# w2 in 27 rows for every partition, and two more rows for the first 64 partitions

## The chip, the cores and the metric

The kernel runs on one core of a Trainium2 chip. The metric is the device time of one execution in microseconds (us); the time of the kernel before is the median of three runs. One execution more was taken with the hardware profiler; the profile, the trace behind it and all times inside the program come from that one.

## What is computed

One token for each of four sequences goes through a transformer layer in bfloat16: attention over the last 2048 positions of a cache, with 32 query heads on 4 key-value heads, then a gated feed-forward part. Cut to what matters:

```python
# x [4,1,1024]; wq [1024,4096]; wo [4096,1024]; w1, w3 [1024,3584]; w2 [3584,1024]
q = layernorm(x) @ wq                       # 32 heads of 128
p = softmax(q . k_cache[last 2048] * 128 ** -0.5)
h = x + (p . v_cache[last 2048]) @ wo
n = layernorm(h)
out = h + (silu(n @ w1) * (n @ w3)) @ w2
```

Each weight and each used row of the caches is read once, and there are only four rows of activations, so most of the work is moving 55.58 MB from HBM to SBUF.

## The kernel before

**Loads.** All large loads go through a ring of five slots of 32 KB for each partition (`NSLOT`, `SLOT`). The list `ring` (L107) gives their order: k in two pairs, half of wq, two slots without a load (for the transposed k), the other half of wq, v in two pairs, wo in two pairs, w1 in two halves, w3 in two halves, w2. `fill()` (L119 to L135) runs down this list and issues each load on SyncE's queue at L133, as far as the slot that it needs was released; `done()` marks a part as used and calls `fill()` again. So the loads stand in one queue in this order, and SyncE waits in it for what the slot's former readers have to finish. The order of all other instructions is the order in which the program writes them (`manual_schedule`).

**Layout of the weights.** wq, w1, w3 have row `p * 8 + kc` on partition p, four `kc` to a load. w2 has row `p * 28 + fc` on partition p (`w2_v`, L79), 28 rows for each, and is loaded in four transfers of 16, 8, 2 and 2 rows (`W2B`, L108): the first fills a slot, the other three share the last one. wo comes as four transfers of 2 MB (`wo_`, L101), two to a slot.

**Attention** (L234 to L424). TensorE transposes k; the projection by wq is made in four bands of 32 partitions (`tile_position`); then scores, row maxima, exponentials on ScalarE, a transpose of the weights on VectorE, and the product with v, pipelined over the four sequences.

**From wo to the end.** L434 multiplies with wo, 128 matmuls of 256 columns; L444 adds x; a second layernorm gives `hn_T`. `up_projection` (L450 to L466) makes for w1 and again for w3 64 matmuls of 448 columns: 8 `kc`, two halves `hf` of the columns, four bands `c`. Band c holds the columns `c * 896` to `c * 896 + 895`, so the result is two tiles of 128 x 448. L472 to L476 make silu of the first result from exp, add, reciprocal and multiply, before the second projection; L480 multiplies it with the second result. `transpose_quads` (L223) transposes the 128 x 896 product in 32 x 32 blocks on VectorE into `hg_T`, 28 blocks of 32 columns. L491 multiplies block fc with row fc of every partition's w2: 112 matmuls of 256 columns, which accumulate in one PSUM tile. L501 adds h, and two small transfers store the result, one on SyncE's queue and one on ScalarE's (L503, L504).

Of the kernel before, what the change touches and what calls it, by code (L numbers as in the profile page):

```python
# [10 lines left out]
P = 128  # L11
ACT = mybir.ActivationFunctionType
ALU = mybir.AluOpType
AX = mybir.AxisListType
BF16 = mybir.dt.bfloat16
FP32 = mybir.dt.float32
# [7 lines left out]
def kernel(  # L24
# [20 lines left out]
    nc = tc.nc  # L45

    B, _, D = A_x.shape
    Hkv, Sk, Dh = A_k_cache.shape[1], A_k_cache.shape[2], A_k_cache.shape[3]
    NQ = A_wq.shape[1]
    Hq = NQ // Dh  # L50
    REP = Hq // Hkv
    W = min(4096, max(256, Sk // 4))
    F = B_w1.shape[1]
    KC = D // P
    FC = F // P
    NK = W // P
    C = 4
    R = 32
    S = R // B
    DQ = D // C  # L60
    FQ = F // C
    FH = FQ // 2
    assert B == C and Hkv == C and B * Hq == P and Dh == P and REP * Hkv == R
    assert D == KC * P and F == FC * P and W == NK * P and NQ == Hq * Dh
    eps = 1e-5
    qscale = float(Dh) ** -0.5

# [3 lines left out]
    T = REP  # L71
# [4 lines left out]
    wo_v = A_wo.rearrange("(g p t) n -> p g (t n)", g=Hkv, t=T)  # L76
    w1_v = B_w1.rearrange("(p kc) f -> p kc f", kc=KC)
    w3_v = B_w3.rearrange("(p kc) f -> p kc f", kc=KC)
    w2_v = B_w2.rearrange("(p fc) n -> p fc n", fc=FC)  # L79

    const = ctx.enter_context(tc.tile_pool(name="const", bufs=1))
    act = ctx.enter_context(tc.tile_pool(name="act", bufs=1))
# [3 lines left out]
    ps = ctx.enter_context(tc.tile_pool(name="ps", bufs=1, space=bass.MemoryType.PSUM))  # L86
# [6 lines left out]
    def pair(parts):  # L93
        return [parts[0:2], parts[2:4]]
# [3 lines left out]
        for name, cache in (("k", A_k_cache), ("v", A_v_cache))  # L98
    )
    kT_ = pair([("kT", b, [JR, P], None) for b in range(B)])  # L100
    wo_ = pair([("wo", g, [1, T * D], wo_v[:, g : g + 1, :]) for g in range(Hkv)])  # L101

    def four_rows(name, view, n):
        return [[(name, i, [4, n], view[:, 4 * i : 4 * i + 4, :])] for i in range(KC // 4)]

    wq_ = four_rows("wq", wq_v, NQ)
    ring = k_ + wq_[:1] + kT_ + wq_[1:] + v_ + wo_ + four_rows("w1", w1_v, F) + four_rows("w3", w3_v, F)  # L107
    W2B = [16, 8, 2, 2]  # L108
    w2_ = []
    f0 = 0  # L110
    for i, n in enumerate(W2B):
        w2_.append(("w2", i, [n, D], w2_v[:, f0 : f0 + n, :]))
        f0 += n
    ring += [w2_[:1], w2_[1:]]
    views = {}
    taken = []
    used = set()
# [1 line left out]
    def fill():  # L119

        while len(taken) < len(ring):
            n = len(taken) - NSLOT
            if n >= 0 and not all((name, i) in used for name, i, _, _ in ring[n]):
                break
            parts = ring[len(taken)]
            slot = stream.tile([P, SLOT], BF16, tag="slot", name="s_" + parts[0][0])
            o = 0
            for name, i, shape, src in parts:
                dst = slot[:, o : o + int(np.prod(shape))]
                o += int(np.prod(shape))  # L130
                view = dst.rearrange("p (a b) -> p a b", a=shape[0])
                if src is not None:
                    nc.sync.dma_start(out=dst if name in ("k", "v") else view, in_=src)  # L133
                views[(name, i)] = view
            taken.append(slot)  # L135

    def get(name, i):
        return views[(name, i)]

    def done(name, i):  # L140
        used.add((name, i))
        fill()
# [5 lines left out]
    nc.vector.memset(x_nat[:], 0.0)  # L148
    nc.scalar.dma_start(out=x_nat[::S, :], in_=x_flat.rearrange("b (c n) -> c b n", c=C))
    fill()  # L150

    ident = const.tile([P, P], BF16)
# [8 lines left out]
        out=t32[:], in_=ident[:].rearrange("p (q h) -> p h q", q=C), axis=AX.X, op=ALU.add  # L161
# [4 lines left out]
    for q in range(C):  # L166
# [3 lines left out]
        out=negm[:], in_=t32[:].rearrange("p (g r) -> p g r", g=Hkv), axis=AX.X, op=ALU.add  # L170
    )
    nc.vector.tensor_scalar(
        out=negm[:], in0=negm[:], scalar1=-1.0, scalar2=-NEG, op0=ALU.add, op1=ALU.mult
# [3 lines left out]
        out=jmask[:, :, 0], in_=ident[:].rearrange("p (j h) -> p j h", j=JM), axis=AX.X, op=ALU.add  # L177
# [6 lines left out]
    for l in range(2):  # L184
        nc.gpsimd.tensor_copy(
            out=strip[:, l, B - 1 :].rearrange("p (c x) -> p c x", c=C)[:, :, : B * Hkv].rearrange(
                "p c (g b) -> p c g b", b=B
            )[:, :, :, 0],
            in_=t32[:].rearrange("p (g c l) -> p l c g", g=Hkv, c=C)[:, l],
        )  # L190

    def layernorm_T(h_T, tag):

# [29 lines left out]
    def transpose_quads(dst, src, n):  # L223

        nc.vector.transpose(
            out=dst.rearrange("p j r -> p (j r)"), in_=src.rearrange("p (q j) -> p j q", j=n)
        )
# [24 lines left out]
    for i in range(KC // 4):  # L252
        w = get("wq", i)
        for kk in range(4):
            kc = 4 * i + kk
            for hf in range(2):
                for c in range(C):
                    o = (2 * c + hf) * HALF * Dh
                    nc.tensor.matmul(  # L259
                        q_ps[hf][R * c : R * c + R],  # L260
                        lhsT=xn_T[:, kc, :],
                        rhs=w[:, kk, o : o + HALF * Dh],
                        start=(kc == 0),
                        stop=(kc == KC - 1),
                        tile_position=(0, R * c),
# [12 lines left out]
    for b in range(B):  # L278
        nc.vector.tensor_copy(  # L279
            out=Qm[:, b].rearrange("p (g y) -> p g y", y=QW)[:, :, :REP],  # L280
            in_=qT_ps[:, :, :, S * b].rearrange("p r g -> p g r"),
# [125 lines left out]
    for l in range(2):  # L407
        for b in range(B):
            nc.tensor.matmul(  # L409
                on_ps[:, l],  # L410
                lhsT=strip[:, l, B - 1 - b : B - 1 - b + P],
                rhs=om[:, b],
                start=(b == 0),
                stop=(b == B - 1),
# [8 lines left out]
        out=oP[:, :, :, ::S],  # L423
        in_=oX[:, :, : Hkv * B].rearrange("p t (g b) -> p g t b", b=B),  # L424
# [2 lines left out]

    y_ps = ps.tile([P, DQ], FP32, tag="kt0")
    for g in range(Hkv):
        w = get("wo", g)  # L430
        for t in range(T):
            for c in range(C):
                o = t * D + c * DQ
                nc.tensor.matmul(  # L434
                    y_ps[R * c : R * c + R, :],
                    lhsT=oP[:, g, t, :],
                    rhs=w[:, 0, o : o + DQ],
                    start=(g == 0 and t == 0),
                    stop=(g == Hkv - 1 and t == T - 1),
                    tile_position=(0, R * c),  # L440
                )
        done("wo", g)
    h1 = act.tile([P, DQ], FP32)
    nc.vector.tensor_tensor(out=h1[:], in0=y_ps[:], in1=x_nat[:], op=ALU.add)  # L444
    h_T = act.tile([P, KC, R], FP32)
# [1 line left out]
    hn_T = layernorm_T(h_T[:], "ln2")  # L447


    def up_projection(name, out_ps):  # L450
        for i in range(KC // 4):
            w = get(name, i)
            for kk in range(4):
                kc = 4 * i + kk
                for hf in range(2):
                    for c in range(C):
                        o = c * FQ + hf * FH
                        nc.tensor.matmul(  # L458
                            out_ps[hf][R * c : R * c + R],
                            lhsT=hn_T[:, kc, :],  # L460
                            rhs=w[:, kk, o : o + FH],
                            start=(kc == 0),
                            stop=(kc == KC - 1),
                            tile_position=(0, R * c),
                        )
            done(name, i)  # L466

    gu_ps = [ps.tile([P, FH], FP32, tag=f"sc{i}", name=f"gu_ps{i}") for i in range(4)]
    up_projection("w1", gu_ps[:2])
    eg = act.tile([P, 2, FH], FP32)  # L470
    for hf in range(2):
        nc.scalar.activation(out=eg[:, hf], in_=gu_ps[hf][:], func=ACT.Exp, scale=-1.0)  # L472
    nc.vector.tensor_scalar_add(out=eg[:], in0=eg[:], scalar1=1.0)
    nc.vector.reciprocal(out=eg[:], in_=eg[:])
    for hf in range(2):
        nc.vector.tensor_tensor(out=eg[:, hf], in0=gu_ps[hf][:], in1=eg[:, hf], op=ALU.mult)  # L476
    up_projection("w3", gu_ps[2:])
    hg = act.tile([P, 2, FH], BF16)
    for hf in range(2):
        nc.vector.tensor_tensor(out=hg[:, hf], in0=gu_ps[2 + hf][:], in1=eg[:, hf], op=ALU.mult)  # L480
    hg_T = act.tile([P, FC, R], BF16)
    transpose_quads(hg_T[:], hg[:].rearrange("p a f -> p (a f)"), FC)


    y2_ps = ps.tile([P, DQ], FP32, tag="kt1")
    fc = 0
    for i, n in enumerate(W2B):
        w = get("w2", i)
        for ff in range(n):
            for c in range(C):  # L490
                nc.tensor.matmul(  # L491
                    y2_ps[R * c : R * c + R, :],
                    lhsT=hg_T[:, fc, :],
                    rhs=w[:, ff, c * DQ : (c + 1) * DQ],
                    start=(fc == 0),
                    stop=(fc == FC - 1),
                    tile_position=(0, R * c),
                )
            fc += 1
    res = act.tile([P, DQ], BF16)  # L500
    nc.vector.tensor_tensor(out=res[:], in0=y2_ps[:], in1=h1[:], op=ALU.add)  # L501
    out_v = out_flat.rearrange("b (c n) -> c b n", c=C)
# [32 lines left out]
```

## Time and profile before

| what | value |
|---|---|
| time, median of 3 runs (lowest to highest) | 140.02 us (139.83 to 140.04) |
| the profiled execution's own time | 140.13 us |
| its span, first to last instruction | 138.3 us |
| its time outside the span | 1.83 us |
| read from HBM | 55.58 MB, 402 GB/s over the span |
| busy: PE, DVE, ACT, POOL | 80.2, 52.9, 42.7, 4.2 us |
| mean granted clock of TensorE | 0.781 |

How to read what follows. PE is TensorE's matmuls and PEld its weight loads, DVE is VectorE, ACT ScalarE, POOL GpSimd, SP SyncE; a q behind a name is the engine's instruction queue. The page cuts the span into 40 equal slices; a digit is a busy share in tenths, and GB/s is what the DMA engines moved in that slice. Queue lines give packets, MB and the share of sixteen DMA engines' span that the packets took. The chain that ended last is followed back from the last instruction; a row of it has start, length, engine and tile. A row of the timeline has start, length, engine, line, operation, output and inputs, shapes, number of instructions, and in brackets how long the engine stood idle before and what ended that. Behind the views stand the trace's single packets (queue, start, length, bytes) and, for each transfer, the times at which its closing signals arrived, one for each DMA engine that took part.

### The profile page before, as it was taken

The numbers are of one execution on the slowest core, as the hardware profiler recorded it, in microseconds if no ns is written. First come the engines' busy times: TensorE is split into PE (matmuls) and PEld (weight loads), VectorE is DVE, ScalarE is ACT, GpSimd is POOL, SyncE is SP. The second block draws the span as 40 slices with busy tenths as digits, with TensorE's granted clock in tenths as the row PEclk, the third lists the DMA queues.
The fourth block names the chain that finished last, engine by engine and source line by source line (L and its number), as shares of the span: only waits on it lengthen the run. The fifth ranks groups of instructions, "written<-read, shape, count | busy, mean of one in ns | idle before, by whom it ended". The sixth has DMA issues, their size and how long they took to land.

```text
span 138.3 us, 2012 instructions
## 1 busy us (share of the span) xinstructions
PE 80.2 (58%) x866; PEld 47.5 (34%) x868; DVE 52.9 (38%) x97; ACT 42.7 (31%) x57; POOL 4.2 (3%) x18
## 2 busy tenths in 40 slices
PE   0029898921903889328918998659539901703780
PEld 0029887820301322014304434537324400202550
DVE  3036676520000235177087197540330298350001
ACT  3005988850000325998807900000040200000000
POOL 7400000000000000000000000000000000000000
PEclk9999999998555799975797799965865896555555
DMA  4999999999989999999999999999999999999930
GB/s 152 399 423 431 431 436 455 455 441 398 445 384 426 441 417 417 450 407 431 450 400 431 433 469 431 394 448 448 419 398 448 456 411 430 445 407 398 406 148 2
DMA packets 3217, 55.72 MB, mean 403 GB/s; under 512 B 360, under 2 KB 392, under 8 KB 648
## 3 DMA queue, kind: packets, MB, share of 16 engines
q1 hardware_dynamic: 3178, 55.58, 94.4%
q8 instruction: 7, 0.11, 0.3%
q10 hardware_dynamic: 30, 0.01, 0.0%
q14 instruction: 2, 0.02, 0.0%
HBM read 55.58 MB, written 0.01 MB: 402 GB/s over the span
## 4 chain that ended last, share of the span: by engine, by line
DMA 49%; PE 27%; DVE 13%; ACT 4%; SPq 3%; issue 2%; DVEq 0%
DMA s_wq<-in_A_wq_dram 29%; DMA s_w<-in_B_w_dram 20%; PE o_ps L369 10%; PE y_ps L434 5%; ACT P L334 4%; PE sc_ps L294 3%; DVE PT L346 3%; SPq L133 3%; PE gu_ps L458 2%; PE q_ps L259 2%; DVE om L386 2%; DVE od L378 2%; PE on_ps L409 1%; PE tot_ps L355 1%; PE nm_ps L323 1%
## 5 line engine op out<-in xcount | busy, mean ns | idle before, releaser
L334 ACT ACTIVATE P<-sc_ps,bias 128x512 bf16<-128x512 f32 x16 | 19.7, 1417 | 9.6 <-DVE bias L331 9.6
L241 PE MATMUL kt_ps<-ident,s_k 128*128 128x128 bf16 x256 | 17.3, 228 | 1.3 <-ACT s_kT L245 1.0
L369 PE MATMUL o_ps<-s_v,PT 128*128 128x512 bf16 x62 | 17.5, 439 | 0.3 <-issue 0.2
L241 PEld LDWEIGHTS <-s_k 128*128 128x128 bf16 x256 | 16.3, 103 | 2.3 <-issue 1.7
L245 ACT COPY s_kT<-kt_ps 128x1024 bf16<-128x1024 bf16 x16 | 15.7, 1012 | 2.5 <-PE kt_ps L241 2.5
L458 PE MATMUL gu_ps<-s_w,n_T 128*32 128x448 bf16 x128 | 10.7, 513 | 8.8 <-DMA s_w<-in_B_w_dram 6.8
L259 PE MATMUL q_ps<-s_wq,n_T 128*32 128x512 bf16 x64 | 7.0, 615 | 11.8 <-DMA s_wq<-in_A_wq_dram 11.8
L243 DVE COPY s_kT<-kt_ps 128x1024 bf16<-128x1024 bf16 x16 | 11.1, 693 | 5.8 <-PE kt_ps L241 5.8
L491 PE MATMUL y_ps<-s_w,hg_T 128*32 128x256 bf16 x112 | 6.6, 418 | 8.0 <-DMA s_w<-in_B_w_dram 8.0
L369 PEld LDWEIGHTS <-PT 128*128 128x128 bf16 x64 | 7.2, 117 | 9.2 <-issue 4.4
L346 DVE STREAM_TRANSPOSE PT<-P 128x2048 bf16<-128x2048 bf16 x4 | 9.2, 2303 | 2.7 <-ACT P L334 2.7
L208 ACT ACTIVATE rstd<-rstd,eps_t 128x4 f32<-128x4 f32 x2 | 0.6, 297 | 29.5 <-DVE rstd L207 29.5
L458 PEld LDWEIGHTS <-n_T 128*32 128x32 bf16 x128 | 4.7, 131 | 14.1 <-issue 11.6
L294 PE MATMUL sc_ps<-s_kT,Qm 128*32 128x512 bf16 x64 | 8.5, 603 | 0.4 <-DVE Qm L279 0.4
L491 PEld LDWEIGHTS <-hg_T 128*32 128x32 bf16 x112 | 4.9, 142 | 10.0 <-issue 5.9
L259 PEld LDWEIGHTS <-n_T 128*32 128x32 bf16 x64 | 2.7, 137 | 15.6 <-issue 15.5
L269 DVE CAST q_sb<-q_ps 128x512 bf16<-128x512 f32 x1 | 0.7, 692 | 18.3 <-PE q_ps L259 18.3
L198 PE MATMUL sums_ps<-both,ones_f 128*128 128x64 f32 x4 | 1.1, 373 | 11.2 <-DVE both L196 11.2
L434 PE MATMUL y_ps<-s_wo,oP 128*32 128x256 bf16 x128 | 6.5, 397 | 1.7 <-DVE oP L422 1.7
L378 DVE SCALAR_TENSOR_TENSOR od<-o_ps,rinv,jmask 128x512 f32<-128x512 f32 x4 | 3.0, 751 | 8.4 <-PE o_ps L369 8.3
L270 ACT CAST q_sb<-q_ps 128x512 bf16<-128x512 f32 x1 | 0.6, 585 | 17.8 <-PE q_ps L259 17.8
L310 PE MATMUL mx_ps<-ident_f,rmax 128*1 128x128 f32 x8 | 1.7, 302 | 7.4 <-DVE rmax L308 7.4
(68 smaller groups left out, 64.7 us busy)
## 6 DMA issues: line engine op xcount, KB each, us to landing
s_w<-in_B_w_dram SPq DMA_DIRECT2D x4, 3584.0 KB, 21.2
s_k<-in_A_k_cache_dram SPq DMA_DIRECT2D x4, 2048.0 KB, 16.1
s_wq<-in_A_wq_dram SPq DMA_DIRECT2D x2, 4096.0 KB, 35.3
s_v<-in_A_v_cache_dram SPq DMA_DIRECT2D x4, 2048.0 KB, 25.1
s_wo<-in_A_wo_dram SPq DMA_DIRECT2D x4, 2048.0 KB, 25.5
s_w<-in_B_w_dram SPq DMA_DIRECT2D x1, 4096.0 KB, 28.0
s_w<-in_B_w_dram SPq DMA_DIRECT2D x1, 2048.0 KB, 25.7
s_w<-in_B_w_dram SPq DMA_DIRECT2D x2, 512.0 KB, 27.0
```

Of the source, the lines that this page charges most:

```text
L241: nc.tensor.transpose(out=kt_ps[:, jj], in_=k[:, jb * JB + jj, :], identity=ident[:])
L243: nc.vector.tensor_copy(out=kT[:, jb * JB : (jb + 1) * JB], in_=kt_ps[:])
L245: nc.scalar.copy(out=kT[:, jb * JB : (jb + 1) * JB], in_=kt_ps[:])
L259: nc.tensor.matmul(q_ps[hf][R * c : R * c + R], lhsT=xn_T[:, kc, :], rhs=w[:, kk, o : o + HALF * Dh], start=(kc == 0), stop=(kc == KC - 1) ...
L294: nc.tensor.matmul(sc_ps[b][R * q : R * q + R], lhsT=Qm[:, b, g * R : (g + 1) * R], rhs=v[:, g, q], start=(g == 0), stop=(g == Hkv - 1), t ...
L334: nc.scalar.activation(out=P4[:, :, :, g], in_=sc_ps[b][:].rearrange("p (j i) -> p j i", i=L5), func=ACT.Exp, bias=bias[:, g : g + 1], sca ...
L346: nc.vector.transpose(out=PT[:].rearrange("p j h -> p (j h)"), in_=stage.pop(("P4", b))[:].rearrange("p j i g -> p (j i g)"),)
L369: nc.tensor.matmul(o_ps[:], lhsT=PT[:, i * JM : (i + 1) * JM, :].rearrange("p j h -> p (j h)"), rhs=v[:, i * JM : (i + 1) * JM, :], start= ...
L378: nc.vector.scalar_tensor_tensor(out=od[:], in0=o_ps[:], scalar=rinv[:, 0:1], in1=jmask[:].to_broadcast([P, JM, Dh]), op0=ALU.mult, op1=AL ...
L434: nc.tensor.matmul(y_ps[R * c : R * c + R, :], lhsT=oP[:, g, t, :], rhs=w[:, 0, o : o + DQ], start=(g == 0 and t == 0), stop=(g == Hkv - 1 ...
L458: nc.tensor.matmul(out_ps[hf][R * c : R * c + R], lhsT=hn_T[:, kc, :], rhs=w[:, kk, o : o + FH], start=(kc == 0), stop=(kc == KC - 1), til ...
L491: nc.tensor.matmul(y2_ps[R * c : R * c + R, :], lhsT=hg_T[:, fc, :], rhs=w[:, ff, c * DQ : (c + 1) * DQ], start=(fc == 0), stop=(fc == FC ...
```

## The change

w2's 3584 rows are split. The first 3456 stand 27 to a partition, so that the third-last transfer has seven rows for every partition where it had eight. The last 128 rows become a tile `w2x` of two rows on each of the partitions 0 to 63, put at the start of the last slot and loaded ahead of the seven-row transfer. Its source is written with an outermost dimension of eight and a stride, its destination is 64 partitions of 4 KB; the transfer takes eight DMA engines. Row `16 i + 2 e + y` of these 128 goes to partition `8 e + i`.

The columns of w1 and w3 follow this split. Each band has 864 columns in two halves of 432, and the last 128 columns go into a third PSUM tile: two bands of 64 columns, each a strided view. That is 16 more matmuls in each projection. The gate's steps each get a third, small part of 64 partitions and 64 columns; add and reciprocal run over 928 columns where they ran over 896. A second, small transpose makes `hx_T`. The product with w2 has 27 steps with all partitions and, behind the first 16, two steps with 64 partitions. A memset on GpSimd, early in the program, fills the part of `eg` that has no data.

wo is loaded in two transfers of 4 MB where there were four of 2 MB; both have the same 16 KB pieces, and the slots are the same.

```diff
-    FC = F // P
+    FC = F // P - 1
+    FM = FC * P
+    XP = P // 2
+    XR = 2
...
-    FQ = F // C
+    FQ = FM // C
     FH = FQ // 2
+    FX = 32 * XR
...
-    w2_v = B_w2.rearrange("(p fc) n -> p fc n", fc=FC)
+    w2_v = B_w2[:FM].rearrange("(p fc) n -> p fc n", fc=FC)
+    w2x_v = B_w2[FM:].rearrange("(i e y) n -> e i (y n)", i=8, e=8)
...
-    wo_ = pair([("wo", g, [1, T * D], wo_v[:, g : g + 1, :]) for g in range(Hkv)])
+    wo_ = [[("wo", i, [2, T * D], wo_v[:, 2 * i : 2 * i + 2, :])] for i in range(Hkv // 2)]
...
-    W2B = [16, 8, 2, 2]
+    W2B = [16, 7, 2, 2]
...
-    ring += [w2_[:1], w2_[1:]]
+    ring += [w2_[:1], [("w2x", 0, [XR, D], w2x_v)] + w2_[1:]]
...
-                if src is not None:
+                if name == "w2x":
+                    nc.sync.dma_start(out=dst[:XP], in_=src)
+                elif src is not None:
...
+    eg = act.tile([P, FQ + FX], FP32)
+    nc.gpsimd.memset(eg[XP:, FQ:], 0.0)
...
     for g in range(Hkv):
-        w = get("wo", g)
+        w = get("wo", g // 2)
...
-                    rhs=w[:, 0, o : o + DQ],
+                    rhs=w[:, g % 2, o : o + DQ],
...
-        done("wo", g)
+        if g % 2 == 1:
+            done("wo", g // 2)
...
+                for c in range(XP // R):
+                    nc.tensor.matmul(
+                        out_ps[2][R * c : R * c + R],
+                        lhsT=hn_T[:, kc, :],
+                        rhs=w[:, kk, FM:].rearrange("p (i c y) -> p c i y", i=8, c=2)[:, c],
+                        start=(kc == 0),
+                        stop=(kc == KC - 1),
+                        tile_position=(0, R * c),
+                    )
...
+    def parts(t, three):
+
+        yield t[:, :FH], three[0][:]
+        yield t[:, FH:FQ], three[1][:]
+        yield t[:XP, FQ:], three[2][:XP]
...
+    for e, g in parts(eg, gate_ps):
+        nc.scalar.activation(out=e, in_=g, func=ACT.Exp, scale=-1.0)
     nc.vector.tensor_scalar_add(out=eg[:], in0=eg[:], scalar1=1.0)
     nc.vector.reciprocal(out=eg[:], in_=eg[:])
...
+    for e, g in parts(eg, gate_ps):
+        nc.vector.tensor_tensor(out=e, in0=g, in1=e, op=ALU.mult)
+    up_projection("w3", up_ps)
+    hg = act.tile([P, FQ + FX], BF16)
+    for (h, u), (e, _) in zip(parts(hg, up_ps), parts(eg, up_ps)):
+        nc.vector.tensor_tensor(out=h, in0=u, in1=e, op=ALU.mult)
     hg_T = act.tile([P, FC, R], BF16)
-    transpose_quads(hg_T[:], hg[:].rearrange("p a f -> p (a f)"), FC)
+    transpose_quads(hg_T[:], hg[:, :FQ], FC)
+    hx_T = act.tile([XP, XR, R], BF16)
+    nc.vector.transpose(
+        out=hx_T[:].rearrange("p y r -> p (y r)"),
+        in_=hg[:XP, FQ:].rearrange("p (i e y) -> p y e i", i=8, e=4),
+    )
...
         for ff in range(n):
...
+            down(hg_T[:, fc, :], w[:, ff], fc == 0, fc == FC - 1)
             fc += 1
+        if i == 0:
+            for y in range(XR):
+                down(hx_T[:, y, :], get("w2x", 0)[:XP, y], False, False)
```

`down` is the loop over the four bands that stood at L490 to L498.

More of the change, by code (lines that the diff above doesn't have):

```diff
@@ L60 @@
     DQ = D // C
-    FQ = F // C
+    FQ = FM // C
     FH = FQ // 2
+    FX = 32 * XR
     assert B == C and Hkv == C and B * Hq == P and Dh == P and REP * Hkv == R
-    assert D == KC * P and F == FC * P and W == NK * P and NQ == Hq * Dh
+    assert D == KC * P and F == FM + XP * XR and W == NK * P and NQ == Hq * Dh
     eps = 1e-5
@@ L465, in up_projection @@
                         )
-            done(name, i)
[L468 to L472, printed above, removed]
+                for c in range(XP // R):
[7 more added lines that the diff above has]
+                    )
@@ new lines, in up_projection @@
+            done(name, i)
+    gate_ps, up_ps = (
+        [
+            ps.tile([P, n], FP32, tag=tag, name=f"{name}_{tag}")
+            for n, tag in zip((FH, FH, FX), tags)
+        ]
+        for name, tags in (("gate", ("sc0", "sc1", "kt2")), ("up", ("sc2", "sc3", "kt0")))
+    )
[3 more added lines that the diff above has]
+        yield t[:XP, FQ:], three[2][:XP]
+    up_projection("w1", gate_ps)
+    for e, g in parts(eg, gate_ps):
+        nc.scalar.activation(out=e, in_=g, func=ACT.Exp, scale=-1.0)
@@ L473 @@
     nc.vector.tensor_scalar_add(out=eg[:], in0=eg[:], scalar1=1.0)
     nc.vector.reciprocal(out=eg[:], in_=eg[:])
[L475 to L480, printed above, removed]
-    hg_T = act.tile([P, FC, R], BF16)
-    transpose_quads(hg_T[:], hg[:].rearrange("p a f -> p (a f)"), FC)
@@ L485 @@
-    y2_ps = ps.tile([P, DQ], FP32, tag="kt1")
+    for e, g in parts(eg, gate_ps):
[4 more added lines that the diff above has]
+        nc.vector.tensor_tensor(out=h, in0=u, in1=e, op=ALU.mult)
+    hg_T = act.tile([P, FC, R], BF16)
+    transpose_quads(hg_T[:], hg[:, :FQ], FC)
[3 more added lines that the diff above has]
+        in_=hg[:XP, FQ:].rearrange("p (i e y) -> p y e i", i=8, e=4),
+    )
@@ L486, with down @@
+    y2_ps = ps.tile([P, DQ], FP32, tag="kt1")
+    def down(lhsT, rows, start, stop):
+        for c in range(C):
+            nc.tensor.matmul(
+                y2_ps[R * c : R * c + R, :],
+                lhsT=lhsT,
+                rhs=rows[:, c * DQ : (c + 1) * DQ],
+                start=start,
+                stop=stop,
+                tile_position=(0, R * c),
+            )
     fc = 0
@@ L489 @@
         for ff in range(n):
[L490 to L498, printed above, removed]
+            down(hg_T[:, fc, :], w[:, ff], fc == 0, fc == FC - 1)
             fc += 1
+        if i == 0:
+            for y in range(XR):
+                down(hx_T[:, y, :], get("w2x", 0)[:XP, y], False, False)
     res = act.tile([P, DQ], BF16)
```

## The prediction

> **What bounds the kernel now.** I read the slices of the page first, then the chain that ended last, then the table of stretches at the end, and last the single packets.
>
> The slices say that the DMA engines never rest between the start and the end:
>
> ```profile
> DMA  4999999999989999999999999999999999999930
> GB/s 152 399 423 431 431 436 455 455 441 398 445 384 426 441 417 417 450 407 431 450 400 431 433 469 431 394 448 448 419 398 448 456 411 430 445 407 398 406 148 2
> q1 hardware_dynamic: 3178, 55.58, 94.4%
> q8 instruction: 7, 0.11, 0.3%
> ```
>
> Only slices 1, 39 and 40 are not full. The 55.58 MB of queue 1 are what SyncE orders at L133; whatever an engine does is paid only if it comes after the last byte. The end of the chain says what that is:
>
> ```profile
> 106.89 27.36 DMA s_w<-in_B_w_dram
> 134.26 0.04 issue
> 134.30 0.64 PE y_ps L491 x8
> 134.94 0.02 issue
> 134.97 0.42 DVE res L501
> ```
>
> The last two rows of w2 land at 134.26 us, and everything after it (eight matmuls, one add, the store) fills the 4.0 us to 138.3. So the time is the moment at which the slowest DMA engine finishes, plus a constant. The stretches (length, busy times of PE, PEld, DVE, ACT, POOL, clock, DMA share, GB/s) show that the engines do not finish together:
>
> ```profile
> 131.00:132.00 1.00, 0.23 (x8) 0.20 (x11) 0.00 (x0) 0.00 (x0) 0.00 (x0) 0.50 0.91 365
> 132.00:133.00 1.00, 1.00 (x24) 0.86 (x20) 0.00 (x0) 0.00 (x0) 0.00 (x0) 0.50 0.52 209
> 133.00:134.00 1.00, 1.00 (x23) 0.70 (x13) 0.00 (x0) 0.00 (x0) 0.00 (x0) 0.50 0.29 111
> ```
>
> By the share, about half of the engines have stopped soon after 132, and a third still work after 133.
>
> The trace keeps start, length and size of every packet but not its engine. Within an engine a packet starts 3 to 4 ns before the one before it ends, so the 3,168 load packets of queue 1 can be linked into sixteen chains of 198. That linking is my reconstruction. The eight chains that start first (2.16 to 2.23 us) hold all four streams of x's load, and end at 131.73, 131.82, 131.85, 131.89, 131.97, 132.00, 132.61 and 133.07. The eight that start later (2.26 to 2.48 us) end at 131.97, 132.31, 133.62, 133.71, 133.74, 133.75, 133.77 and 133.78. The landing itself is seen some 0.48 us after a chain's end. I call them the first and the second eight.
>
> The cause of the late ones is visible: queue 8's 16 KB packets start at 20.5, 29.7, 52.3, 87.4, 100.2 and 112.9 us, and each time one chain of the second eight, each time another, has a hole of 0.99 to 1.09 us. (The seventh, at 133.5, finds an idle engine.) The two late chains of the first eight, 132.61 and 133.07, lost theirs beside queue 14's 8 KB packets at 69.9 and 77.7 us: a hole of 0.31 us and one 16 KB packet of 1273 and 991 ns for 611.
>
> **The change, part by part.** Packet prices from the trace: 4096 bytes take 159 ns, 16384 bytes 611 ns, a transfer's 4-byte closing packet 9 ns; each overlaps its successor by 3.5 ns. A row of 14336 bytes is not there; between the two it is 611 - 2048 x 452/12288 = 536 ns.
>
> *w2's third transfer, seven rows for eight.* Every engine saves 8 x 75 = 0.60 us.
>
> *w2x.* 128 rows of 2 KB are 64 packets of 4 KB, eight for each of eight engines: 8 x 155.5 + 5.5 = 1.25 us on these at an engine's own rate, nothing on the others. That the eight are the first eight is likely: x's load has four outer steps, shows four closing packets, and all four sit in the first eight.
>
> *wo in two transfers for four.* Same packets, two closing packets fewer: 0.01 us less for each engine. Slots come free at the same points. On SP's queue two issues of about 0.6 us go and one comes; from v on, the loads take 21 to 28 us from issue to landing, of which an own transfer time is at most 10, so the queue holds over 10 us of work and no engine runs dry.
>
> Sum at own rate: first eight +1.25 - 0.60 - 0.01 = +0.64, second eight -0.61. The first eight's slowest then ends at 133.07 + 0.64 = 133.71, the second eight's at 133.78 - 0.61 = 133.17. The end moves from 133.78 to 133.71: **0.07 us** gained, not the 0.61 that the second eight gain, because the chain that queue 14 had delayed is now last.
>
> *Does w2x run at that rate?* No row shows a transfer to 64 partitions. All the bulk loads put eight rows on each of sixteen engines, over all 128 partitions; w2x puts eight rows on each of eight engines, over half of them, so engines that never met may meet at a destination. Lower bound: 159 ns, 1.25 us in all. Upper bound: the rows where two streams share one way, the 16 KB data packets beside an instruction fetch, which took 991 to 1273 ns for 611, about double; then w2x takes 2.50 us. If, besides, another engine's w2x meets the late engine's own w2_0 packets, it loses up to 1.25 us again. I take the doubling once: eight engines at full rate into half of the partitions are twice what the loads of before put there, if the place is what limits, and it is the engine that is already late that pays. The late chain then ends at 133.71 + 1.25 = 134.96, which is **1.18 us** after 133.78.
>
> [...]
>
> *PE's, DVE's and ACT's extra work.* Each projection gets 16 matmuls of 64 columns; its 64 others shrink from 448 to 432 columns. At 14 to 56 ns each (the 256-column ones of L491 take 3.61/64 = 56 ns) that is 0.2 to 0.9 us, less 64 x 3.3 ns = 0.2: 0 to 0.7 us. The gate adds one small exp (a 448-column one takes 0.49 us), 32 of 896 columns to add and reciprocal (6.4 us x 3.6% = 0.23) and one small multiply (below 0.58); the same again after w3, and one small transpose. What covers it:
>
> ```profile
> 116.14 1.16 DVE L476 TENSOR_TENSOR eg<-gu_ps,eg 128x448 f32<-128x448 f32 x2
> ...
> 117.17 3.18 PE L458 MATMUL gu_ps<-s_w,n_T 128*32 128x448 bf16 x32 [6.81 <-DMA s_w<-in_B_w_dram]
> ...
> 120.02 1.16 DVE L480 TENSOR_TENSOR hg<-gu_ps,eg 128x448 bf16<-128x448 f32 x2 [2.72 <-PE gu_ps L458]
> 121.21 1.70 DVE L225 STREAM_TRANSPOSE hg_T<-hg 128x896 bf16<-128x896 bf16 x1
> ...
> 126.88 3.61 PE L491 MATMUL y_ps<-s_w,hg_T 128*32 128x256 bf16 x64 [6.53 <-DMA s_w<-in_B_w_dram]
> ```
>
> The gate has 120.02 - 117.30 = 2.7 us to spare and would use at most 0.7 + 0.5 + 0.23 + 0.58 = 2.0; after w3, hg_T stands at 122.9 and w2's first rows land at 126.84, 3.9 us of cover for at most 0.7 + 0.6 + 0.6. The net four extra matmuls of L491's kind (8 for w2x, 4 fewer for the row) cost 0.23 us and fall into PE's wait from 130.5 to 131.77. Memset on POOL: in the first 4 us, behind loads. All nothing. Without that cover each would be paid in full.
>
> *The seventh instruction fetch.* The fetches come every 240 PE instructions or so; 64 more before the last stage bring the seventh from 133.5 to between 129 and 133 us, when engines still load, at 1.0 to 1.1 us for the one it hits. The six before took six different chains of the second eight; its other two end after the change at 131.36 and 131.70 and can bear it. On a chain of the first eight it would add up to 1.1 us.
>
> [...]
>
> **Rivals.** (1) *Own rate, late first-half chain stays*: -0.07 us, 139.95. For it: every packet of a size has one length here, whatever the others do. (2) *Faster*: queue 14's packets hit other engines than in this execution, or its two chains are not of the eight. The place is the end of w2; first eight then end at 132.0 + 0.64 = 132.64, second at 133.17: -0.61, 139.4. It decides as long as w2x costs under 1.25 + 0.53 = 1.78 us an engine. Against it: x's packets tie both late chains to the first eight. (3) *w2x falls on late engines of the second eight*, or the seventh fetch on a busy engine: 133.78 + 0.64 = 134.42, +0.64, 140.7. (4) *It does not do what it says* and takes sixteen engines: bytes balanced as before, within 0.05 us, 140.0.
>
> **The numbers.** The forecast (shared place, 0.60): span 138.3 + 1.18 = 139.48, with the 1.83 us around it 141.31 in the profiled execution, whose 140.13 stands 0.11 above the median: **141.2**. Of its 0.60, 0.03 stay within 0.2% (0.28 us, about what can be told from no change). Rival 1: 0.15; 2: 0.17; 3: 0.05; 4: 0.03. Faster 0.17, same 0.03 + 0.15 + 0.03 = 0.21, slower 0.57 + 0.05 = 0.62. The range goes from within the faster case, 139.5, to nearly the double sharing (136.21, +2.43, 142.45), 142.3; the likeliest case alone spans 140.2 (a fifth of w2x shared: +0.25 - 0.07) to 142.4.
>
> **What would show it.** Right: w2x's 4 KB packets about 310 ns instead of 159, the last landing near 135.4, stretches before it with a few engines of the first eight still loading. Wrong: packets at 159 ns and the last landing at 134.2 (rival 1) or 133.65 (rival 2). The eight added packets missing on some chains and the chains' ends show rivals 3 and 4. If w2's first matmuls wait for DVE and not for DMA, my cover was wrong.

## The result and the profile after

The changed kernel takes 142.31 us, median of 6 runs (141.97 to 142.7), beside 140.01 for the kernel before (139.83 to 140.06): ratio 1.0169, 95% interval 1.015 to 1.0189. That is 2.30 us slower, where 1.18 had been forecast, and 0.01 us above the range. Its profiled execution took 142.7 us with a span of 140.8.

The slices of the changed kernel, to be held beside those of before: the DMA engines are as full as they were, but three slices near the end move far less.

```profile
DMA  3999999999999999999999999999999999999920
GB/s 149 411 420 437 433 437 447 410 424 447 447 414 414 428 433 428 419 424 437 435 419 414 467 415 424 461 407 424 464 404 424 464 425 428 428 280 308 378 100 2
q1 hardware_dynamic: 3218, 55.58, 94.0%
```

Slices 36, 37 and 38 stand at 280, 308 and 378 GB/s, where the kernel before has 407, 398 and 406. The bytes are the same 55.58 MB. The busy share is at 9 tenths in all three: with fewer GB/s the packets take longer, and the engines do not wait for work. What is missing, (127 + 90 + 28) GB/s over slices of 3.52 us, is 0.86 MB, at 420 GB/s about 2 us of the whole stream.

The end of the chain of the changed kernel:

```profile
110.65 26.12 DMA s_w2x<-in_B_w_dram
136.78 0.04 issue
136.82 0.64 PE y_ps L528 x8
137.46 0.02 issue
137.48 0.42 DVE res L547
```

The last landing moved from 134.26 to 136.78 us, by 2.52; the same eight matmuls, add and store follow. So all of the time is in when the last bytes land. The stretches (length, PE, PEld, DVE, ACT, POOL, clock, DMA share, GB/s) say when it was lost. First the kernel before, then the changed one:

```profile
122.00:124.00 2.00, 0.00 (x0) 0.10 (x1) 0.91 (x1) 0.00 (x0) 0.00 (x0) 0.50 1.07 459
124.00:126.00 2.00, 0.00 (x0) 0.00 (x0) 0.00 (x0) 0.00 (x0) 0.00 (x0) 0.50 0.77 328
126.00:128.00 2.00, 1.12 (x24) 0.98 (x27) 0.00 (x0) 0.00 (x0) 0.00 (x0) 0.50 0.96 410
128.00:130.00 2.00, 2.00 (x44) 1.75 (x40) 0.00 (x0) 0.00 (x0) 0.00 (x0) 0.50 1.02 432
```

```profile
122.00:124.00 2.00, 0.00 (x0) 0.10 (x1) 1.49 (x2) 0.00 (x0) 0.00 (x0) 0.50 1.04 442
124.00:126.00 2.00, 0.00 (x0) 0.00 (x0) 0.00 (x0) 0.00 (x0) 0.00 (x0) 0.50 0.98 258
126.00:128.00 2.00, 0.00 (x0) 0.00 (x0) 0.00 (x0) 0.00 (x0) 0.00 (x0) 0.50 0.90 216
128.00:130.00 2.00, 1.81 (x36) 1.59 (x39) 0.00 (x0) 0.00 (x0) 0.00 (x0) 0.50 0.90 302
130.00:132.00 2.00, 2.00 (x44) 1.26 (x35) 0.00 (x0) 0.00 (x0) 0.00 (x0) 0.57 0.99 416
```

In the kernel before, share and rate fall together (0.77 and 328); in the changed one the share stays at 0.98 and 0.90 while the rate goes to 258 and 216. The rate falls with w2x's first packets at 124 us and is back at 416 after 130 us.

The single packets name who is slow. Between 124.2 and 130 us, in the changed kernel's trace:

| packets | normal length, ns | over 1.15 times normal | mean of those, ns | longest, ns |
|---|---|---|---|---|
| 4096 bytes (w2x) | 159 | 48 of 64 | 286 | 465 |
| 14336 bytes (w2, seven rows) | 536 | 53 of 74 | 869 | 1167 |
| 32768 bytes (w2, first 16 rows) | 1214 | 7 of 7 | 2092 | 2202 |

Of the 145 packets 108 take longer, on average 1.6 to 1.8 times their normal length, and not only on the engines that carry w2x. The chains are the prediction's: packets linked by their times, one chain for each engine. Two of them go from the first 16 rows straight to the seven rows, so w2x is not on them, and their packets of 536 ns take 568, 906 and 1107, and 595, 907 and 1105 ns. Before, not one load packet after 122 us was longer than 1.15 times its normal length.

The cover that the prediction named held, though attention ran later in this execution (h is added at 101.67 us for 98.84, where DMA does not wait for it). The timeline of the changed kernel:

```profile
119.37 1.12 DVE L510 TENSOR_TENSOR eg<-gate_sc,eg 128x432 f32<-128x432 f32 x2
120.41 0.21 DVE L510 TENSOR_TENSOR eg<-gate_kt,eg 64x64 f32<-64x64 f32 x1
120.54 1.10 DVE L514 TENSOR_TENSOR hg<-up_sc,eg 128x432 bf16<-128x432 f32 x2
121.70 1.63 DVE L237 STREAM_TRANSPOSE hg_T<-hg 128x864 bf16<-128x864 bf16 x1
123.26 0.23 DVE L518 STREAM_TRANSPOSE hx_T<-hg 64x64 bf16<-64x64 bf16 x1
128.19 3.61 PE L528 MATMUL y_ps<-s_w,hg_T 128*32 128x256 bf16 x64 [8.58 <-DMA s_w<-in_B_w_dram]
```

The two small steps take 0.21 and 0.23 us, everything is ready at 123.5, and PE then waits for DMA until 128.19.

### The profile page after: what moved, and what is told of

The parts are those of the page before. It is cut to its first block, busy times and chain, and to the rows that moved or that the text cites. A ratio compares the mean times of both kernels' runs of the same rounds, so it can differ in the third digit from the quotient of the medians.

```text
span 140.8 us, 2090 instructions
## 1 busy us (share of the span) xinstructions
PE 84.2 (60%) x904; PEld 51.3 (36%) x904; DVE 53.2 (38%) x100; ACT 43.3 (31%) x58; POOL 4.4 (3%) x19
## 3 DMA queue, kind: packets, MB, share of 16 engines
q1 hardware_dynamic: 3218, 55.58, 94.0%
HBM read 55.58 MB, written 0.01 MB: 395 GB/s over the span
## 4 chain that ended last, share of the span: by engine, by line
DMA 47%; PE 29%; DVE 13%; ACT 4%; SPq 3%; issue 2%; DVEq 0%
DMA s_wq<-in_A_wq_dram 28%; DMA s_w2x<-in_B_w_dram 19%; PE o_ps L381 11%; PE y_ps L446 5%; ACT P L346 4%; PE sc_ps L306 3%; DVE PT L358 3%; SPq L142 3%; PE gate_sc L471 2%; PE q_ps L271 2%; DVE om L398 2%; DVE od L390 2%; PE tot_ps L367 1%; PE nm_ps L335 1%; PE on_ps L421 1%
## 5 line engine op out<-in xcount | busy, mean ns | idle before, releaser
L381 PE MATMUL o_ps<-s_v,PT 128*128 128x512 bf16 x64 | 19.4, 471 | 0.0
L253 PE MATMUL kt_ps<-ident,s_k 128*128 128x128 bf16 x256 | 19.1, 238 | 0.4
L253 PEld LDWEIGHTS <-s_k 128*128 128x128 bf16 x256 | 17.7, 109 | 1.8 <-issue 1.1
L257 ACT COPY s_kT<-kt_ps 128x1024 bf16<-128x1024 bf16 x16 | 16.2, 1012 | 2.9 <-PE kt_ps L253 2.0
L381 PEld LDWEIGHTS <-PT 128*128 128x128 bf16 x64 | 7.7, 126 | 10.3 <-issue 6.5
L528 PEld LDWEIGHTS <-hg_T 128*32 128x32 bf16 x108 | 4.1, 126 | 13.2 <-issue 8.5
L528 PE MATMUL y_ps<-s_w,hg_T 128*32 128x256 bf16 x64 | 3.6, 417 | 8.6 <-DMA s_w<-in_B_w_dram 8.6
L471 PEld LDWEIGHTS <-n_T 128*32 128x32 bf16 x128 | 5.3, 121 | 8.0 <-issue 4.7
L271 PEld LDWEIGHTS <-n_T 128*32 128x32 bf16 x64 | 2.7, 138 | 14.8 <-issue 14.7
L471 PE MATMUL gate_sc<-s_w,n_T 128*32 128x432 bf16 x64 | 6.0, 547 | 1.9 <-DVE n_T L230 1.9
L471 PE MATMUL up_sc<-s_w,n_T 128*32 128x432 bf16 x64 | 4.3, 392 | 3.9 <-DMA s_w<-in_B_w_dram 3.9
```

Of the source, the lines that this page charges most:

```text
L253: nc.tensor.transpose(out=kt_ps[:, jj], in_=k[:, jb * JB + jj, :], identity=ident[:])
L257: nc.scalar.copy(out=kT[:, jb * JB : (jb + 1) * JB], in_=kt_ps[:])
L271: nc.tensor.matmul(q_ps[hf][R * c : R * c + R], lhsT=xn_T[:, kc, :], rhs=w[:, kk, o : o + HALF * Dh], start=(kc == 0), stop=(kc == KC - 1) ...
L381: nc.tensor.matmul(o_ps[:], lhsT=PT[:, i * JM : (i + 1) * JM, :].rearrange("p j h -> p (j h)"), rhs=v[:, i * JM : (i + 1) * JM, :], start= ...
L471: nc.tensor.matmul(out_ps[hf][R * c : R * c + R], lhsT=hn_T[:, kc, :], rhs=w[:, kk, o : o + FH], start=(kc == 0), stop=(kc == KC - 1), til ...
L528: nc.tensor.matmul(y2_ps[R * c : R * c + R, :], lhsT=lhsT, rhs=rows[:, c * DQ : (c + 1) * DQ], start=start, stop=stop, tile_position=(0, R ...
```

## The experiments

**Is it the place that w2x is written to?** Theory A, after the prediction: engines meet at w2x's destination, and what meets there holds up the others too. This is the author's estimate. That engine j writes partitions 8j to 8j+7 is assumed, here and in the expectations, and so is which partitions make up one place; the trace shows neither. The rival, B: the way w2x is read, or the use of eight engines.

*e1_own_place.* Same bytes from the same addresses, with the same outermost dimension of eight, but in two transfers of 32 partitions; by the assumed placing engine e writes partitions 4e to 4e+3 and then 32+4e to 32+4e+3:

```diff
-                    nc.sync.dma_start(out=dst[:XP], in_=src)
+                    for h in range(2):
+                        nc.sync.dma_start(out=dst[R * h : R * h + R], in_=src[:, 4 * h : 4 * h + 4])
...
-                        rhs=w[:, kk, FM:].rearrange("p (i c y) -> p c i y", i=8, c=2)[:, c],
+                        rhs=w[:, kk, FM + c * FX : FM + (c + 1) * FX],
...
-        in_=hg[:XP, FQ:].rearrange("p (i e y) -> p y e i", i=8, e=4),
+        in_=hg[:XP, FQ:].rearrange("p (i e y) -> p y e i", i=4, e=8),
```

> The same 256 KB, the same eight engines, the same 4 KB pieces from the same addresses, but w2x goes in two transfers of 32 partitions, so that each engine writes only its own groups of four partitions (4e to 4e+3, then 32+4e to 32+4e+3); the matching columns of w1 and w3 are taken in order. Theory A (engines of w2x meet at their destination, and what meets there holds up the others too): packets back to 159 ns, last landing near 134.2 us, time 139.9 to 140.1. Theory B (the way w2x is read, or that only eight engines take part, holds everything up): no change against the changed kernel, 142.3.

Measured: 140.27 us, ratio 1.0024 (1.0015 to 1.0033). Two of the 2.3 us are gone. Its stretches:

```profile
124.00:126.00 2.00, 0.00 (x0) 0.00 (x0) 0.00 (x0) 0.00 (x0) 0.00 (x0) 0.50 0.78 327
126.00:128.00 2.00, 1.05 (x24) 0.88 (x27) 0.00 (x0) 0.00 (x0) 0.00 (x0) 0.50 0.95 401
128.00:130.00 2.00, 2.00 (x44) 1.69 (x40) 0.00 (x0) 0.00 (x0) 0.00 (x0) 0.50 1.01 428
```

They are those of the kernel before. w2x's packets take 161 ns on average, none over 171. The loss goes with the destination, as A said, and B falls; but the time is 0.2 to 0.3 us above what A said, which the second group of experiments takes up.

*e11_two_that_meet*, the control: two transfers as well, but on even and odd partitions, so that every byte goes where the changed kernel puts it.

```diff
-                    nc.sync.dma_start(out=dst[:XP], in_=src)
+                    for h in range(2):
+                        nc.sync.dma_start(out=dst[h:XP:2], in_=src[:, h::2])
```

> The changed kernel with w2x in two transfers of 32 partitions, as in e1_own_place, but on the even and then the odd ones of the partitions 0 to 63: every byte goes where the changed kernel puts it, and engine j writes partitions 8j to 8j+7 as there. Control for e1_own_place. Theory A (the destination): 142.0 to 142.6. If splitting the transfer in two was what helped e1_own_place: 140.1 to 140.4.

Measured: 142.06 us, 1.0141 (1.0126 to 1.0157). Its stretches:

```profile
124.00:126.00 2.00, 0.00 (x0) 0.00 (x0) 0.00 (x0) 0.00 (x0) 0.00 (x0) 0.52 0.93 267
126.00:128.00 2.00, 0.17 (x5) 0.14 (x7) 0.00 (x0) 0.00 (x0) 0.00 (x0) 0.50 0.96 273
128.00:130.00 2.00, 2.00 (x44) 1.74 (x40) 0.00 (x0) 0.00 (x0) 0.00 (x0) 0.50 0.92 343
```

The fall in the rate is back. From e1_own_place this run differs in the destination and, with it, in the order of the eight pieces under each index of the outermost dimension; the changed kernel has them in e1_own_place's order and is slow. So neither the split nor the order is the cause: the destination is. What meets there was not separated: packets of w2x with each other, or with those of the other loads. Nor did a run show why the one placing is slow and the other is not.

*e4_w2x_sixteen.* A plain load of the same rows, meant for sixteen engines, again to 64 partitions:

```diff
-    w2x_v = B_w2[FM:].rearrange("(i e y) n -> e i (y n)", i=8, e=8)
+    w2x_v = B_w2[FM:].rearrange("(p y) n -> p (y n)", y=XR)
```

with the columns in order as in e1_own_place and the transpose's input as `"p (j y) -> p y j"`.

> w2x as a plain load: partition p takes the two rows 2p and 2p+1, so the source is one run of 256 KB and the transfer can take sixteen engines with four 4 KB packets each; the destination is again 64 partitions. A: two engines meet on each group of partitions, so packets slower than 159 ns while it lasts and a loss, but at most that of the changed kernel: 140.8 to 142.3. B: 159 ns a packet, bytes level as before, 140.0 to 140.2.

Measured: 142.0 us, 1.014 (1.0123 to 1.0157), with 99 packets over 1.15 times normal. So the loss does not need a source with an outermost dimension of eight: this load to 64 partitions is 2.03 us above the 139.97 of the kernel before as well.

*e7_upper_half.* w2x to the other 64 partitions:

```diff
-                    nc.sync.dma_start(out=dst[:XP], in_=src)
+                    nc.gpsimd.memset(dst[:XP], 0.0)
+                    nc.sync.dma_start(out=dst[XP:], in_=src)
```

> The changed kernel with w2x written to partitions 64 to 127, the 64 partitions that are read being zeroed on GpSimd instead (the part of the result from those rows is missing). Theory A (engines that meet on one group of partitions): the same pairs meet in the other half, 141.8 to 142.8, with slow packets on nearly all chains. If the loss came from partitions 0 to 63 or their own engines in particular: below 141.

Measured: 142.74 us, 1.0189 (1.0174 to 1.0203). The loss is there in the other half too.

**What does it cost, and whom?** *e2_no_w2x* has `nc.gpsimd.memset(dst[:XP], 0.0)` in place of w2x's transfer.

> The changed kernel without the load of w2x: the 128 rows are replaced by zeros written on GpSimd, so their share of the result is left out. If w2x alone makes the loss (A and B): every engine moves 16 KB less than before and the second eight end last at 133.17 us, so 139.4 (139.2 to 139.6). If the 27-row layout, the seven-row transfer or the added matmuls make it: above 141.5.

Measured: 139.33 us, 0.9954 (0.9941 to 0.9968), as forecast: the last landing is at 133.67 us, where 133.17 for the chain and 0.48 for the landing had been expected. The end of its chain:

```profile
106.79 26.88 DMA s_w2x<-in_B_w_dram
133.67 0.04 issue
133.71 0.43 PE y_ps L528 x8
```

The 27-row layout and the added work on PE, DVE and ACT cost nothing. So w2x costs 142.31 - 139.33 = 2.98 us. Some 0.2 us of it may be TensorE's clock: in the profiled execution the last eight matmuls took 0.43 us at a granted clock of 1.00, and 0.64 us at 0.50 in the kernel before and in the changed one. At the stream's rate of about 420 GB/s the 256 KB of w2x are 0.62 us; in e1_own_place they cost 140.27 - 139.33 = 0.94 us.

*e3_wo_only* gives the kernel before the two wo transfers.

> The kernel before, with only wo loaded in two transfers of 4 MB for four of 2 MB. A and B: 140.0, within 0.2 us, no slow packets. If the loss came from here: above 141.

Measured: 139.96 us, 0.9997 (0.9988 to 1.0007). Nothing.

*e10_half* loads and uses one row of w2x's two.

```diff
-                    nc.sync.dma_start(out=dst[:XP], in_=src)
+                    nc.sync.dma_start(out=dst[:XP, :D], in_=src[:, :, :D])
...
-            for y in range(XR):
+            for y in range(1):
```

> The changed kernel with only the first of w2x's two rows loaded and used for each of its 64 partitions (64 rows of the product are missing): 2 KB pieces, 128 KB. e2_no_w2x stands at 139.33 and the changed kernel at 142.3, so w2x costs 2.97. If the price goes with the bytes that meet: 139.33 + 1.5 = 140.8 (140.5 to 141.2). If it is a price for each packet or for the transfer, whatever its size: 141.8 to 142.3.

Measured: 140.87 us, 1.006 (1.0046 to 1.0073): 1.54 us above e2_no_w2x, 0.52 of the 2.98. The price goes with the bytes; the packets of w2x are 64 in both.

*e8_early* loads w2x into a tile of its own ahead of w1 (`nc.sync.dma_start(out=w2x_t[:XP], in_=w2x_v)`) and has `bufs=2` for `ptpool`, which makes room.

> The changed kernel with w2x loaded into a tile of its own ahead of w1 (near 78 us), still by eight engines to 64 partitions; one buffer fewer for the transposed weights of attention. Theory A1 (while engines meet, all sixteen move less, and a stream that is never idle cannot catch up): the same 2.3 us are lost in mid-stream, 141.8 to 142.6. A2 (only engines that meet pay, and the loss showed because it came at the end): the last stages run as without sharing, 139.9 to 141.2.

Measured: 141.84 us, 1.0139 (1.0118 to 1.0159). Its stretches in mid-stream:

```profile
76.00:80.00 4.00, 4.00 (x11) 1.46 (x10) 1.54 (x3) 4.00 (x8) 0.00 (x0) 0.54 1.00 424
80.00:82.00 2.00, 2.00 (x12) 1.11 (x11) 0.70 (x1) 1.46 (x3) 0.00 (x0) 1.00 0.99 320
82.00:84.00 2.00, 1.95 (x10) 0.88 (x9) 1.97 (x3) 0.00 (x0) 0.00 (x0) 1.00 1.15 344
84.00:86.00 2.00, 1.29 (x8) 0.55 (x7) 1.86 (x4) 0.00 (x0) 0.00 (x0) 1.00 0.98 416
```

The dip stands at 80 to 84 us, with over 50 us of work behind it, and 1.8 us stay lost: a stream without a pause did not make up for it. It is 0.5 us less than at the end, of which part may be that no tail is late in addition; that was not separated, and the smaller `ptpool` was not run by itself.

**Why is e1_own_place not at the own-rate sum of 139.95?** In its profiled execution the seventh instruction fetch, at 132.4 us, fell on a chain that carried w2x's packets; that chain ended at 134.27, its like at 132.65 to 132.78, and the chain beside queue 14 at 133.63, where the prediction had 133.71. The theory was that the seventh fetch is the difference.

*e5_own_place_less_pe* is e1_own_place with fewer PE instructions ahead of the end:

```diff
-        for t in range(T):
+        for t in range(T if g < Hkv - 1 else 1):
```

> e1_own_place with 28 of the 128 wo matmuls left out (a part of the result is missing): about 56 PE instructions fewer ahead of the last stages. In e1_own_place the seventh instruction fetch starts at 132.4 us on a chain of the first eight that is still loading and ends last, at 134.27 where its neighbours end near 132.7. If that fetch is the whole difference between e1_own_place and the forecast at own rate: the fetch comes after 133 us to an idle engine, the last chain is the one beside queue 14 at 133.6, time 139.9 to 140.0. If e1_own_place is slower for another reason: 140.2 to 140.3 as before.

Measured: 140.25 us, 1.0012 (1.0002 to 1.0022): a miss for the median. But the one profiled execution took 139.63, the eleven others 140.14 to 140.46.

*e9_no_seventh* has `range(T if g == 0 else 0)` there.

> e1_own_place with 96 of the 128 wo matmuls left out (a large part of the result is missing): about 192 PE instructions fewer, so that the seventh instruction fetch should not come at all and the sixth comes late. e5_own_place_less_pe left the median at 140.25 although its one profiled execution, in which the fetch hit an idle chain, took 139.63. If a seventh fetch on a loading chain is what stands between e1_own_place and the own-rate forecast: 139.6 to 140.0, below the kernel before. If not: 140.2 to 140.3.

Measured: 140.34 us, 1.0017 (1.0006 to 1.0028). The seventh fetch is gone from the trace, and the time is not: the theory falls. What the trace shows in its place: the fetches at 30.7 and 53.2 us stand in two chains that carry w2x, where the prediction had all of the early fetches on chains without it, and these two end last, at 134.10. One of the eleven executions took 139.6.

*e12_second_look* is e5_own_place_less_pe again, for a second profile of one program.

> The program of e5_own_place_less_pe once more, for a second profiled execution. Its first took 139.63 us, with all six early instruction fetches on chains without w2x, while its eleven other executions took 140.14 to 140.46. If the engine that a fetch takes changes from execution to execution, and this makes the difference: most likely 140.1 to 140.5, and then a fetch's hole of about 1 us stands in a chain that also carries w2x's eight packets, and that chain ends last. If fetches always take the same engines: 139.6 and the same chains.

Measured: 140.29 us. The ends of the two chains, first e5_own_place_less_pe, then this one:

```profile
134.00 0.04 issue
134.04 0.45 PE y_ps L529 x8
134.49 0.02 issue
134.51 0.42 DVE res L548
```

```profile
134.54 0.04 issue
134.58 0.64 PE y_ps L529 x8
135.22 0.02 issue
135.24 0.42 DVE res L548
```

In the first all six early fetches stand in chains without w2x (ends 132.79 to 132.97), and the last chain is the one beside queue 14, at 133.52. In the second the sixth fetch, at 120.8 us, stands in a chain with w2x, which ends last at 134.06. So the engine of an instruction fetch was not the same in these two executions of one program (they ran on two chips), and in the second one fetch made a w2x chain the last, at 134.06 for 133.52.

*e6_less_pe* takes the same 28 matmuls from the changed kernel.

> The changed kernel with the same 28 wo matmuls left out. There the fetch at 133.5 us delays a chain that ends at 135.9, not the last one at 136.3. If the meeting at the destination makes the end: no change, 142.0 to 142.5. If the fetch makes part of the loss: 141.0 to 141.8.

Measured: 142.38 us, 1.0169 (1.0146 to 1.0192). So the seventh fetch decides nothing there. An earlier one does, in the profiled execution: the chain that ends last, at 136.18 us, carries w2x and had been delayed by one of the first six fetches. It starts its part of w2x at 126.94 us; the chains without a delay start theirs at 124.4 to 124.8. The next chain ends at 135.39.

## Why the prediction was right and where it failed

**Right.** The bound (last landing plus a constant): the constant was 4.0 us in both. The direction, and that w2x's destination is the reason: shown by e1_own_place and e11_two_that_meet against the changed kernel. That engines meet there is the author's estimate; no run shows the meeting. Loads to 64 partitions took 2.03 us more than the kernel before with other source rows for each partition (e4_w2x_sixteen) and 2.67 more in the upper half (e7_upper_half). The own-rate ends of the chains, with w2x left out or at 161 ns a packet: 133.17 and 133.71 forecast, 133.26 in e2_no_w2x and 133.63 in e1_own_place. wo and the work on PE, DVE and ACT at nothing: e3_wo_only and e2_no_w2x.

**Failed: the price of w2x.** "I take the doubling once [...] it is the engine that is already late that pays": the step let each w2x engine lose 1.25 us on its own eight packets, and set the end by one late chain, 1.18 us after before's. Measured, w2x's packets took 1.6 times their length on average (255 ns for 159), but those of the other engines were slowed as much, as long as w2x lasted (on a chain without w2x 568, 906 and 1107 ns for 536, 1.6 times): from e2_no_w2x, w2x costs 2.98 us where the step had 1.18 + 0.61 = 1.79. The step applied the slowing to the wrong set: to eight engines for 1.25 us, not to the whole stream for as long as w2x was in it.

The chains' ends show the size. Chains without w2x and without a fetch end at 133.1 to 133.4 us in the changed kernel, and chains without a fetch or a delay by queue 14 at 131.1 to 131.7 in e2_no_w2x: about 1.9 us for engines that the step let off free. The chain that the prediction named, with w2x and queue 14's longer delay, ends at 135.75, which is 2.04 us after its own-rate 133.71 and not 1.25. Two chains end later: one that the seventh fetch hit, at 135.88, and the last, at 136.30, which carries w2x and was hit by the sixth fetch (the packet behind the fetch's hole, at 115.68 us, takes 1756 ns for 1214, and its w2x starts at 126.81). So in the profiled execution, which at 142.7 us is the slowest of the six, 0.55 us come from the place of the fetches and not from w2x. The upper end of the range, "another engine's w2x meets the late engine's own w2_0 packets", had the size (2.43) by a narrower reason, and the range was cut below it.

The doubling was the author's estimate; no run shows two engines that halve each other's rate at one place. The runs show 2.98/1.79 = 1.7 times what the step summed, and that the loss comes with the destination (142.31 us, and 142.06 in e11_two_that_meet) and goes with it (140.27 in e1_own_place); why all engines are held stays open.

**Failed: the fixed order of the chains.** Rival 1's sum of -0.07 us rests on fetches that fall on chains without w2x, because the one profile of before showed them so. That is one execution. For the kernel before it should matter little, since its chains carry the same bytes; this is argued, not shown. With 32 KB of w2x on eight of the chains it matters. Of the 34 executions of e1_own_place, e5_own_place_less_pe and e9_no_seventh two took 139.6 and the others 140.1 to 140.5, so the medians are 0.2 to 0.3 us above before and not 0.07 below. That the engines of the fetches are the reason was seen in the four that have a profile; of the others it is inferred. The price of a fetch was also too low: the prediction took the hole of 1.0 to 1.1 us, but the packet behind the hole is 0.46 to 0.55 us longer as well, so a fetch costs its chain about 1.5 us (in the kernel before, chain ends of 133.6 to 133.8 against 131.7 to 132.3 where nothing delayed them). Of the 0.66 us between 139.63 and 140.29 of one program, 0.54 are the later landing behind such a fetch; the last eight matmuls add 0.19, at a granted clock of 0.50 for 0.77.

The rivals 2 and 4 did not come; rival 3's seventh fetch came in e1_own_place, but is one case among several. No variant that computes everything was faster than the kernel before: 139.33 was only reached without w2x.

## What to carry to other kernels

Here a stream of loads that kept all engines full was slowed as a whole by a small transfer, and its destination decided how much: 256 KB to 64 partitions cost 2.98 us, and 0.94 when the same rows went to these partitions in another order, in two transfers of 32. Try another placing of the same bytes, and look for the sign: a full DMA share with falling GB/s (0.98 and 258 here, where the kernel before has 0.77 and 328), and packets of known size that take longer on all chains. Before moving load from late engines to early ones, look in more than one execution whether the late ones are the same.

## What was not expected of the hardware

- Packets on chains that carry no w2x take up to 2.1 times their length beside it (1107 ns for 536).
- After the first 12 us, and away from w2x and the packets of queues 8 and 14, a packet of the loads over all 128 partitions has one length for a size, within 8% in both profiles: 159, 536, 611, 1066 and 1214 ns for 4, 14, 16, 28 and 32 KB.
- Each of the first six 16 KB instruction fetches leaves a hole of 1.0 to 1.1 us in one engine's load stream and makes the packet behind it 0.46 to 0.55 us longer, and two executions of one program had a fetch on different engines.
